# An attention block and a channel mix on one core: the opening reordered, one operand loaded instead of computed, all stores in quarters

## The chip, the cores and the metric

One Trainium2 chip, one of its cores. A core has five engines with queues of their own: TensorE (PE, with its weight loads shown as PEld), VectorE (DVE), ScalarE (ACT), GpSimd (POOL) and SyncE (SP). SP, ACT and POOL can issue DMAs. The metric is the device time of one execution in microseconds, a median over runs.

## The reference

Four batches, four heads, 1088 positions, 32 numbers a head. `S1` and `S2` are 8 x 32.

```python
def phi(x):                                   # 64 features of a position
    a = einsum('rd,bhsd->bhsr', S1, x)
    b = einsum('rd,bhsd->bhsr', S2, x)
    return einsum('bhsi,bhsj->bhsij', a, b).reshape(*x.shape[:-1], 64)
q_p, k_p = phi(q), phi(k)
kv  = einsum('bhsf,bhsd->bhfd', k_p, v)
z   = sum(k_p, axis=2)
num = einsum('bhsf,bhfd->bhsd', q_p, kv)
den = einsum('bhsf,bhf->bhs', q_p, z)[..., None] + 1e-06
x   = (num / den), heads side by side         # (4, 1088, 128)

x_prev = x shifted by one position, zero first
xk = mu_k * x + (1 - mu_k) * x_prev
xr = mu_r * x + (1 - mu_r) * x_prev
k  = maximum(xk @ w_k, 0)                     # 128 -> 1024
out = sigmoid(xr @ w_r) * (k * k @ w_v)       # 1024 -> 128
```

## The kernel before

The scheduling is by hand. A text, `ORDER`, lists some 365 tasks; a loop at the end (L601) calls the function of each name in that order, and each engine then works through its own instructions strictly in the order in which they were written. So moving a word in `ORDER` moves that task on its engine's queue, and no other thing plans the work. The parts of a word: `abw.1.0.W@0` is task `abw` for batch 1, half 0, in form `W`, into PSUM bank 0. A last letter A, V or G names ACT, DVE or POOL (in `st` also S for SP); `^sq.1.3.V` adds a wait for that earlier task. Waits follow from the data, PSUM banks included.

The tasks by batch `b`, in the order of the data:

- `kturn.b.y` (DVE, L262) transposes half `y` of k in blocks of 32; `smk`/`sevk` (PE L209, DVE L213) build `SK`, a block form of S1 and S2; `kproj.b.j` (PE, L273) projects k, in form P with 32 columns an instruction or W with 64; `abev` copies to SBUF; `kp.b.j.G` (POOL, L255) makes the 64 features; `kvmm` (PE, L321) sums features times v, then `kvev`, `kdmm`, `kvcp` turn the sums.
- `zmm`, `zev`, `wmm`, `wsq` (PE L300, copy, PE L308, DVE L312) make the denominators' weights from the projections of k, with an operand `ZL`. `ZL` is S1 spread over 128 partitions times a mask: `smz` (PE, L201) spreads S1 by a product with `ez`, and `sevz` (DVE, L204) applies the mask.
- `qturn.b` (DVE, L344) transposes q; `abw.b.g` (PE, L353 and L367; P or W) projects it in two halves, with the denominators' part; `abwev` copies; `pw` (POOL), `dred` (DVE, L393), `drec` (DVE, L398) and `an` (POOL) make and apply the denominators; `qp.b.g` (DVE) makes q's features.
- Batch 0 turns them on PE (`qt`, L473, copied by `qtev`; `qtt`, `qttev`, `xt`, `xtev` for a rest of two positions) and multiplies by kv in `xmh` (PE, L485; copied by `xev`). Batches 1 to 3 turn them on DVE (`qf`, L420) and use `xmm` (PE, L433).
- `xs` (POOL, L498) fills the shifted rows, `xk` and `xkt` (DVE, L505, L464) mix x with x_prev into bf16, `xb` (POOL, L252) makes the other mix's input. `wkc`, `wrc`, `wvc` (POOL) make the bf16 weights; `mumm` and `wmu` turn the mu vectors into columns.

The channel mix runs in nine groups, two a batch (0 to 7) and group 8 of half the size for the rests. `f1.g.c` (PE, L526) makes a quarter of the 1024 hidden rows, two products of 128x512; `relu` (L534 on ACT, L536 on DVE) and `sq` (L546 on ACT, L255 elsewhere) follow; `f2.g.c` (PE, L558) multiplies back; `rr` (PE, L571) and `sig` (ACT, L576) make the gate; `fin` (DVE, L581) multiplies; `st` (L595) stores 256 KB a group, either whole or in quarters of 32 partitions (64 KB).

`zz.n` (PE, L188) issues `n` products of a zero tile with 512 columns of zeros; nothing reads their result.

All loads are issued ahead, on SP but for the first S1 and k half and the two mu rows, which are on ACT, in the order of `LOADS`.

Of the kernel before, what the change touches and what calls it, by code (L numbers as in the profile page):

```python
# [44 lines left out]
kvmm.3.0@5 abwev.3.1.A qf.1.2 relu.1.0.A pw.3.2.G^sq.0.1.V kdmm.1 f1.1.1@01 kvcp.1.A f1.0.3@34 sq.1.0.G relu.1.1.A
kvmm.3.1 dred.3.2.V kproj.2.0.P@6 relu.0.3.A kvev.3.V drec.3.2 kdmm.3 abev.2.0.V rr.0@0 sq.0.2.A an.3.2.G kvcp.3.V
zmm.2@1 kp.2.0.G qp.3.0 xmm.1@3456 sig.0 zev.2.A sq.1.1.A qp.3.1 wmm.2 f2.0.0@7 xev.1.0.A f2.0.1 xtev.1.A wsq.2
xev.1.1.V rr.1@0 sq.1.2.A xs.1 f1.1.3@12 sq.0.3.V abw.2.0.W@3 xk.1.2 relu.1.3.A abw.2.1.W@4 abwev.2.0.A sig.1 sq.1.3.V
f1.3.0@56 abwev.2.1.A qf.3.2 f2.0.2 relu.3.0.A pw.2.2.G^sq.1.3.V f1.2.0@01 f2.1.0@2 xb.1.G^sq.1.3.V relu.2.0.A
f1.3.1@56 f2.0.3 relu.3.1.A f2.1.1 dred.2.2.V f1.3.2@01 fin.0 st.0.S sq.3.0.A f1.2.1@56 drec.2.2 relu.3.2.V f2.1.2  # L50
an.2.2.G relu.2.1.A f2.1.3 kp.2.1.G kvmm.2.0@7 qp.2.0 sq.3.2.A xmm.3@0156 sq.2.0.A fin.1 st.1.S sq.3.1.G qp.2.1
kvmm.2.1 xev.3.0.A f1.3.3@23 xev.3.1.A xtev.3.V f2.3.0@4 kvev.2.V relu.3.3.A xs.3 f1.2.2@56 xk.3.2 f1.2.3@01
relu.2.2.A f2.3.1 rr.3@2 sq.2.1.V relu.2.3.A kdmm.2 f1.6.0@56 sq.2.2.V f2.3.2 relu.6.0.A sq.3.3.V f1.6.1@01 qf.2.2
f2.2.0@3 sq.2.3.G^sq.3.3.V sig.3 f2.3.3 relu.6.1.A f1.7.0@56 f2.2.1 relu.7.0.A rr.2@2 xb.3.G f1.6.2@01 fin.3 st.3.S
kvcp.2.A f2.2.2 relu.6.2.A xmm.2@4567 sq.6.0.V sig.2 sq.7.0.V sq.6.1.V f2.2.3 xev.2.0.A f2.6.0@2 sq.6.2.V xtev.2.A
f1.7.1@01 xev.2.1.A fin.2 st.2.S xs.2^sq.6.2.V f2.6.1 relu.7.1.A xk.2.2 f1.7.2@67 rr.6@3 relu.7.2.A f1.6.3@45 sq.7.1.V
f1.7.3@01 sig.6 f2.6.2 sq.7.2.G^sq.7.1.V relu.7.3.V relu.6.3.A f1.5.0@67 f2.7.0@3 f2.7.1 relu.5.0.A f1.5.1@01 sq.6.3.V
f1.5.2@45 relu.5.1.A rr.7@6 sq.7.3.V f2.6.3 sq.5.0.V sig.7 f1.4.0@01 relu.5.2.V f2.7.2 sq.5.1.G^sq.5.0.V relu.4.0.A
f2.7.3 f1.5.3@67 fin.6 st.6.S sq.5.2.A f1.4.2@45 relu.5.3.V f1.4.1@12 xb.2.G relu.4.2.A f2.5.0@0 f2.5.1 fin.7 st.7.S
relu.4.1.A f1.4.3@67 sq.5.3.V f1.8.0@45 f2.5.2 sq.4.0.V relu.8.0.A f1.8.2@12 f2.5.3 relu.4.3.A sq.4.1.V rr.5@3  # L60
sq.4.2.V rr.8@4 relu.8.2.A f2.4.0@5 sq.8.0.V f1.8.1@67 sig.5 sq.4.3.V f2.4.1 relu.8.1.A f1.8.3@12 sq.8.2.V rr.4@3
fin.5 st.5.0.S st.5.1.S st.5.2.S relu.8.3.A sq.8.1.G^sq.8.2.V f2.4.2 sig.4 f2.4.3 sq.8.3.A f2.8.0@0 fin.4 st.4.0.S
st.4.3.S f2.8.1 sig.8 f2.8.2 f2.8.3 fin.8 st.8.2.S st.5.3.G st.4.1.A st.4.2.G st.8.0.A st.8.1.G st.8.3.A
# [583 lines left out]
```

## Time and profile before

| | |
|---|---|
| median of 3 runs | 81.73 us (81.45 to 82.52) |
| profiled execution | 82.54 us |
| its span, first to last instruction | 80.7 us |
| PE busy | 74.1 us (92%) |
| DVE busy | 65.4 us (81%) |
| ACT busy | 56.0 us (69%) |
| POOL busy | 47.4 us (59%) |
| zero products | 18, 7.7 us |
| HBM read, written | 7.80 MB, 2.23 MB |

Three stretches can be told apart in the slices of the page. Up to some 27 us loads fill the DMA engines and attention of batch 0 and half of that of batches 1 and 3 is made; from there to about 76 the channel mix runs, with what is left of attention between its products; then the last stores land. In a row of the timeline, the first two numbers are the start and the length in microseconds, then engine, line, operation, output<-input, form and count; in brackets stands how long the engine had been idle and what ended that. A row can cover several instructions of the same kind that followed one another. Lines of the chain of waits give start, length and what the time went to.

### The profile page before, as it was taken

The numbers are of one execution on the slowest core, as the hardware profiler recorded it, in microseconds if no ns is written. First come the engines' busy times: TensorE is split into PE (matmuls) and PEld (weight loads), VectorE is DVE, ScalarE is ACT, GpSimd is POOL, SyncE is SP. The second block draws the span as 40 slices with busy tenths as digits, with TensorE's granted clock in tenths as the row PEclk, the third lists the DMA queues.
The fourth block names the chain that finished last, engine by engine and source line by source line (L and its number), as shares of the span: only waits on it lengthen the run. The fifth ranks groups of instructions, "written<-read, shape, count | busy, mean of one in ns | idle before, by whom it ended". The sixth has DMA issues, their size and how long they took to land.

```text
span 80.7 us, 3273 instructions
## 1 busy us (share of the span) xinstructions
PE 74.1 (92%) x1410; PEld 52.2 (65%) x1410; DVE 65.4 (81%) x102; ACT 56.0 (69%) x88; POOL 47.4 (59%) x68
## 2 busy tenths in 40 slices
...
PEclk9999999999999999999999999999999999999995
...
GB/s 20 312 349 307 292 337 362 231 263 310 382 299 245 181 9 0 8 0 12 0 0 12 0 15 71 83 86 24 0 27 96 55 89 0 15 51 109 176 238 5
DMA packets 7258, 10.24 MB, mean 127 GB/s; under 512 B 762, under 2 KB 4060, under 8 KB 7244
## 3 DMA queue, kind: packets, MB, share of 16 engines
...
q10 hardware_dynamic: 308, 0.41, 1.5%
q8 instruction: 11, 0.18, 0.9%
q0 software_dynamic: 96, 0.16, 0.8%
...
HBM read 7.80 MB, written 2.23 MB: 124 GB/s over the span
## 4 chain that ended last, share of the span: by engine, by line
PE 61%; POOL 12%; DVE 10%; ACT 6%; issue 4%; POOLq 1%; ACTq 0%
PE ps L526 13%; PE ps L558 12%; PE ps L188 8%; PE ps L433 6%; PE ps L367 6%; POOL kp L255 5%; PE ps L273 5%; ACT k L534 5%; PE ps L321 3%; DVE k L536 3%; PE ps L571 3%; DVE osb L581 2%; DVE XK L505 2%; DVE k L255 2%; POOL pw L255 1%
## 5 line engine op out<-in xcount | busy, mean ns | idle before, releaser
L534 ACT ACTIVATE k<-ps 128x1024 bf16<-128x1024 f32 (+1 forms) x32 | 29.7, 976 | 1.1 <-DVE XK L505 0.3
L558 PEld LDWEIGHTS <-k 128*128 128x128 bf16 x272 | 16.9, 98 | 4.2 <-issue 0.5
L526 PE MATMUL ps<-XK,wk 128*128 128x512 bf16 (+1 forms) x72 | 19.2, 367 | 0.2 <-DVE XK L464 0.2
L558 PE MATMUL ps<-wv,k 128*128 128x128 bf16 x272 | 19.1, 219 | 0.0
L255 POOL TENSOR_TENSOR kp<-ab 128x1280 f32<-128x1280 f32 (+1 forms) x8 | 17.3, 2178 | 1.0 <-ACT ab L248 1.0
L255 POOL TENSOR_TENSOR k<-k 128x1024 bf16<-128x1024 bf16 (+1 forms) x6 | 10.5, 1751 | 11.8 <-DVE k L255 9.2
L255 DVE TENSOR_TENSOR k<-k 128x1024 bf16<-128x1024 bf16 (+1 forms) x21 | 14.1, 708 | 0.3 <-PE ps L558 0.3
L255 DVE TENSOR_TENSOR qp<-an,ps 128x1152 f32<-128x1152 f32 (+1 forms) x8 | 10.1, 1269 | 0.0
L546 ACT ACTIVATE k<-k 128x1024 bf16<-128x1024 bf16 (+1 forms) x9 | 9.1, 1028 | 0.4 <-PE ps L558 0.3
L188 PE MATMUL ps<-zero 128*128 128x512 bf16 x18 | 7.7, 560 | 1.2 <-DVE warm L155 1.2
L262 DVE STREAM_TRANSPOSE kT<-k 128x576 f32<-128x576 f32 x8 | 5.9, 753 | 3.1 <-DMA k<-in_k_dram 3.1
L526 PEld LDWEIGHTS <-wk 128*128 128x128 bf16 x72 | 6.1, 98 | 3.3 <-issue 0.7
L255 POOL TENSOR_TENSOR pw<-abw 128x272 f32<-128x272 f32 (+2 forms) x5 | 3.3, 650 | 7.6 <-ACT abw L248 7.6
L420 DVE STREAM_TRANSPOSE qf<-qp 128x2176 f32<-128x2176 f32 x3 | 7.3, 2435 | 0.0
L248 ACT COPY ab<-ps 128x256 f32<-128x256 f32 (+1 forms) x7 | 2.7, 396 | 6.1 <-PE ps L273 5.9
L367 PE MATMUL ps<-SQ,qT 128*64 128x96 f32 (+1 forms) x144 | 6.6, 250 | 0.0
L581 DVE TENSOR_TENSOR osb<-ps,r 128x512 f32<-128x512 f32 (+1 forms) x9 | 5.8, 648 | 0.9 <-ACT r L576 0.5
L273 PEld LDWEIGHTS ps<-SK,kT 128*32 128x32 f32 (+1 forms) x200 | 5.3, 145 | 1.4 <-issue 0.8
L273 PE MATMUL ps<-SK,kT 128*32 128x64 f32 (+1 forms) x200 | 6.1, 256 | 0.0
L248 ACT COPY X<-ps 128x512 f32<-128x512 f32 (+2 forms) x12 | 4.9, 434 | 1.8 <-PE ps L485 1.2
L367 PEld LDWEIGHTS ps<-SQ,qT 128*64 128x64 f32 (+1 forms) x144 | 5.5, 131 | 0.5 <-DVE SQ L312 0.3
L321 PE MATMUL ps<-kp,v 128*32 128x64 f32 x288 | 5.7, 222 | 0.0
...
## 6 DMA issues: line engine op xcount, KB each, us to landing
...
```

Source lines behind the costliest of these rows:

```text
L188: nc.tensor.matmul(PS[:, banks[0], :], zero[:, :P], zero[:], skip_group_check=True)
L248: nc.scalar.copy(o, i)
L255: (nc.vector if eng == "V" else nc.gpsimd).tensor_mul(o, a, b)
L273: nc.tensor.matmul(_ap(d, [[n, 2], [1, 32]]), sb["kT", b][:, m, w * c:w * c + w], SK[:, :, :H].rearrange("p x h r -> p x (h r)"), skip_gro ...
L321: nc.tensor.matmul(o[32 * h:32 * h + 32, :F], vin[b][:, h, m, :], sb["kp", b, j][:, 4 * (m - KG[j][0]) + h].rearrange("p i j -> p (i j)"), ...
L367: nc.tensor.matmul(o[32 * w * c:32 * w * c + 32 * w, n:n + 96], sb["qT", b][:, u:u + w, :].rearrange("p u a -> p (u a)"), SQ[b][:, x:x + H ...
L420: nc.vector.transpose(sb["qf", b][:, s0:s1].rearrange("p s f a -> p (s f a)"), sb["qp", b][:, s0:s1].rearrange("p s i j -> p (s i j)"))
L526: nc.tensor.matmul(h[:, c, :], wk[:, P * (2 * cp + c):P * (2 * cp + c) + P], x, skip_group_check=True)
L534: nc.scalar.activation(o, h, RELU)
L546: nc.scalar.activation(o, i, SQUARE)
L558: nc.tensor.matmul(o[:, i * P:i * P + P], k2[:, i * P:i * P + P], wv[:, 2 * cp + c, :], start=(cp == 0 and c == 0 and i == 0), stop=(cp == ...
L581: nc.vector.tensor_mul(o[:].rearrange("p i f -> p (i f)")[:, :n], ps["o", g][:, :n], sb["r", g][:, :n])
```

## The change

- S1 is also loaded once more, read sixteen times over into a tile `SZ` of 128 partitions, by a DMA on ACT's queue behind the first k half and ahead of the mu rows. `sevz` reads `SZ`; the product `smz`, its operand `ez` and the copy that made `ez` go.
- The zero tile has 128 columns instead of 512; the zero product reads it four times over, so that it still has 512 columns. The zero products stand elsewhere: `zz.6 zz.1 zz.4 zz.3 zz.1 zz.3` before, `zz.6 zz.2 zz.1 zz.3 zz.2 zz.4` after.
- `qturn.0` comes before `sevz` and both `kturn.1`, and `abw.0.0` before `kproj.1`.
- The stores of groups 0, 1, 2, 3, 6 and 7 are issued in quarters on SP; those of 5, 4 and 8 were already.
- `ORDER` is new from end to end, with other PSUM banks. Up to the first f1, by engine: DVE `kturn.0.0 kturn.0.1 sevk qturn.0 sevz kturn.1.0 kturn.1.1 wsq.0 dred.0.0 drec.0.0 dred.0.1 qp.0.0 drec.0.1 qturn.1 wsq.1 wmu qp.0.1 kturn.2.0 kturn.2.1 qttev.0 dred.1.2 drec.1.2 qturn.2 kturn.3.0 kturn.3.1 xkt.0 xk.0.0 xk.0.1`; POOL `kp.0.0 kp.0.1 pw.0.0 pw.0.1 an.0.0 kp.1.0 an.0.1 wkc pw.1.2 kp.1.1 wrc wvc an.1.2 xs.0 xb.0`.
- On another engine: ACT to DVE `qttev.0 zev.2 sq.3.0 kvcp.2 relu.8.0`; DVE to ACT `kvev.3 kvev.2 relu.3.2 relu.5.2`; POOL to DVE `sq.7.2 sq.8.1 sq.2.3`; POOL to ACT `sq.3.1`; ACT to POOL `sq.3.2 sq.8.3`; DVE to POOL `sq.2.2`. `kproj.2.0` and `abw.3.0` change from form P to W, `kproj.2.1` from W to P.

```diff
 ORDER = """
-kturn.0.0 zz.6@1 smk@0 smz@1 kturn.0.1 sevk sevz zz.1@2 kproj.0.0.P@0 sqc.2 sqc.1 sqc.0 sqc.3 kproj.0.1.P@1 abev.0.0.A
-kp.0.0.G kturn.1.0 abev.0.1.A zz.4@2 zmm.0@0 kturn.1.1 zev.0.A zz.3@2 wmm.0 qturn.0 kproj.1.1.W@1 kproj.1.0.W@2
-kp.0.1.G wsq.0 zz.1@3 abw.0.0.W@0 abev.1.0.A abev.1.1.A zmm.1@1 abwev.0.0.A abw.0.1.W@2 zev.1.A pw.0.0.G mumm@3
-dred.0.0.V abwev.0.1.A kvmm.0.0@4 drec.0.0 pw.0.1.G qturn.1 an.0.0.G kp.1.1.G qp.0.0 wmm.1 kvmm.0.1 kvev.0.A
-dred.0.1.V zz.3@7 qt.0.0@56 wmu wsq.1 kdmm.0 drec.0.1 qtev.0.0.A abw.1.1.W@3 kturn.2.0 an.0.1.G wrc qtt.0@1 qp.0.1
-abw.1.0.W@0 qttev.0.A kp.1.0.G kvcp.0.A xt.0 kturn.2.1 abwev.1.0.A qt.0.1@45 abwev.1.1.A xtev.0.A xmh.0.0@2 qturn.2
-qtev.0.1.A pw.1.2.G wkc.G xmh.0.1@4 dred.1.2.V drec.1.2 kproj.2.1.W@5 xs.0 kturn.3.0 xev.0.1.A wvc.G kvmm.1.0@6
-abev.2.1.A kturn.3.1 xev.0.0.A an.1.2.G xk.0.0 xb.0.G kproj.3.1.W@5 xkt.0 kproj.3.0.W@7 xk.0.1 abev.3.1.A f1.0.0@12
...
+kturn.0.0 zz.6@1 smk@0 kturn.0.1 sevk zz.2@1 kproj.0.0.P@0 sqc.2 sqc.1 sqc.3 sqc.0 qturn.0 kproj.0.1.P@1 abev.0.0.A
+kp.0.0.G abev.0.1.A sevz kturn.1.0 zz.1@2 zmm.0@0 kturn.1.1 zev.0.A zz.3@2 wmm.0 mumm@1 wsq.0 kp.0.1.G zz.2@2
+abw.0.0.W@0 kproj.1.0.W@2 abwev.0.0.A abw.0.1.W@3 abev.1.0.A pw.0.0.G kproj.1.1.W@4 dred.0.0.V abwev.0.1.A drec.0.0
+pw.0.1.G abev.1.1.A an.0.0.G dred.0.1.V zz.4@5 zmm.1@2 kp.1.0.G qp.0.0 kvmm.0.0@4 zev.1.A kvmm.0.1 drec.0.1 qturn.1
+qtt.0@0 wmm.1 kvev.0.A qt.0.0@56 an.0.1.G wsq.1 wmu kdmm.0 abw.1.0.W@7 qtev.0.0.A qp.0.1 wkc.G abw.1.1.W@1 abwev.1.0.A
+kturn.2.0 qt.0.1@23 abwev.1.1.A kvcp.0.A pw.1.2.G kturn.2.1 kvmm.1.0@4 qtev.0.1.A kp.1.1.G qttev.0.V dred.1.2.V
+drec.1.2 qturn.2 xt.0 xmh.0.1@2 wrc kproj.2.1.P@3 wvc.G xmh.0.0@5 kturn.3.0 abev.2.1.A xtev.0.A an.1.2.G xev.0.1.A
+kturn.3.1 xev.0.0.A xs.0 xkt.0 kproj.3.1.W@3 xk.0.0 xb.0.G kproj.3.0.W@0 xk.0.1 abev.3.1.A f1.0.0@56 abev.3.0.A
...
+    SZ = const.tile([P, D], F32)
...
-    zero = const.tile([P, 512], BF16)
+    zero = const.tile([P, P], BF16)
...
+    nc.scalar.dma_start(SZ[:], dataclasses.replace(S1, ap=[[0, P // R], [D, R], [1, D]]))
...
-    ez = const.tile([R, 16, R], F32)
-    nc.vector.tensor_copy(ez[:], _ap(ident[:R, :R], [[0, 16], [1, R]]))
...
-            nc.tensor.matmul(PS[:, banks[0], :], zero[:, :P], zero[:], skip_group_check=True)
+            nc.tensor.matmul(PS[:, banks[0], :], zero[:], _ap(zero[:], [[0, 4], [1, P]]), skip_group_check=True)
...
-    def smz(banks):
-        ps["sz"] = PS[:, banks[0], :D]
-        nc.tensor.matmul(ps["sz"], ez[:].rearrange("r g j -> r (g j)"), S16[:R, :], skip_group_check=True)
...
-        nc.vector.tensor_mul(ZL[:], _ap(ps["sz"], [[0, 4], [1, D]]), _ap(mz[:], [[1, 4], [0, D]]))
+        nc.vector.tensor_mul(ZL[:], _ap(SZ[:], [[0, 4], [1, D]]), _ap(mz[:], [[1, 4], [0, D]]))
```

More of the change, by code (lines that the diff above doesn't have):

```diff
@@ L40 @@
-abw.1.0.W@0 qttev.0.A kp.1.0.G kvcp.0.A xt.0 kturn.2.1 abwev.1.0.A qt.0.1@45 abwev.1.1.A xtev.0.A xmh.0.0@2 qturn.2
-qtev.0.1.A pw.1.2.G wkc.G xmh.0.1@4 dred.1.2.V drec.1.2 kproj.2.1.W@5 xs.0 kturn.3.0 xev.0.1.A wvc.G kvmm.1.0@6
-abev.2.1.A kturn.3.1 xev.0.0.A an.1.2.G xk.0.0 xb.0.G kproj.3.1.W@5 xkt.0 kproj.3.0.W@7 xk.0.1 abev.3.1.A f1.0.0@12
-qp.1.0 kp.3.1.G abev.3.0.A f1.0.2@45 relu.0.0.A zmm.3@7 kvmm.1.1 zev.3.V qturn.3 relu.0.2.A wmm.3 kp.3.0.G f1.1.2@01
-sq.0.0.A f1.0.1@45 wsq.3 kvev.1.V abw.3.0.P@7 qp.1.1 relu.0.1.A abw.3.1.W@2 abwev.3.0.V relu.1.2.A sq.0.1.V f1.1.0@34
@@ L45 @@
[L45 to L63, printed above, removed]
+kturn.0.0 zz.6@1 smk@0 kturn.0.1 sevk zz.2@1 kproj.0.0.P@0 sqc.2 sqc.1 sqc.3 sqc.0 qturn.0 kproj.0.1.P@1 abev.0.0.A
@@ new lines @@
+drec.1.2 qturn.2 xt.0 xmh.0.1@2 wrc kproj.2.1.P@3 wvc.G xmh.0.0@5 kturn.3.0 abev.2.1.A xtev.0.A an.1.2.G xev.0.1.A
+kturn.3.1 xev.0.0.A xs.0 xkt.0 kproj.3.1.W@3 xk.0.0 xb.0.G kproj.3.0.W@0 xk.0.1 abev.3.1.A f1.0.0@56 abev.3.0.A
+qturn.3 kp.3.1.G f1.0.2@23 relu.0.0.A zmm.3@0 kvmm.1.1 zev.3.V qp.1.0 relu.0.2.A wmm.3 f1.1.2@56 kp.3.0.G sq.0.0.A
+f1.0.1@23 wsq.3 kvev.1.V abw.3.0.W@0 qp.1.1 relu.0.1.A abw.3.1.W@7 relu.1.2.A abwev.3.0.V f1.1.0@12 sq.0.1.V kdmm.1
+abwev.3.1.A qf.1.2 f1.1.1@56 relu.1.0.A pw.3.2.G^sq.0.1.V kvmm.3.0@3 kvcp.1.A kvmm.3.1 sq.1.0.G relu.1.1.A f1.0.3@12
```

22 lines of the change are left out of this document (21 added, 1 removed).

## The prediction

> **What bounds the kernel now.** I read the page first: span, granted clock, the chain that ended last.
>
> ```profile
> span 80.7 us, 3273 instructions
> ...
> PEclk9999999999999999999999999999999999999995
> ...
> PE 61%; POOL 12%; DVE 10%; ACT 6%; issue 4%; POOLq 1%; ACTq 0%
> ```
>
> The chain is PE's for 61% of the span. The busy times by stage say where something else shares the limit (columns: stretch and its length, then busy us and count of PE, PEld, DVE, ACT, POOL).
>
> ```profile
> 27.00:65.00 38.00, 37.85 (x803) 26.77 (x803) 37.30 (x48) 36.28 (x52) 23.19 (x23) 1.00 0.12 33
> 65.00:75.00 10.00, 10.00 (x139) 8.52 (x138) 9.57 (x15) 9.50 (x14) 4.14 (x5) 1.00 0.18 53
> ```
>
> From the first f1 on, PE has 0.15 us free, DVE and ACT 2 to 5% of the time, POOL some 40%. An order can therefore win little there: only what shortens PE's own list, or lets that list begin sooner. So the beginning decides. The timeline, cut to the steps that count (start, length, engine, line, form, idle before):
>
> ```profile
> 5.22 2.15 PE L273 MATMUL ps<-SK,kT 128*32 128x64 f32 x72
> 6.58 0.42 ACT L248 COPY ab<-ps 128x320 f32<-128x320 f32 x1 [2.69 <-PE ps L273]
> 7.26 0.78 DVE L262 STREAM_TRANSPOSE kT<-k 128x576 f32<-128x576 f32 x1 [1.91 <-DMA k<-in_k_dram]
> 7.29 1.89 PE L188 MATMUL ps<-zero 128*128 128x512 bf16 x4
> 7.43 0.37 ACT L248 COPY ab<-ps 128x256 f32<-128x256 f32 x1 [0.43 <-PE ps L273]
> 9.11 0.53 PE L300 MATMUL ps<-ab 128*32 128x32 f32 x18
> 9.13 1.27 DVE L344 STREAM_TRANSPOSE qT<-q 128x1088 f32<-128x1088 f32 x1
> 9.57 1.24 PE L188 MATMUL ps<-zero 128*128 128x512 bf16 x3
> 10.90 1.27 PE L273 MATMUL ps<-SK,kT 128*64 128x64 f32 x36
> 11.01 0.21 DVE L312 TENSOR_TENSOR SQ<-ps,m 128x48 f32<-128x48 f32 x1 [0.61 <-PE ps L308]
> 12.42 0.32 PE L353 MATMUL ps<-SQ,qT 128*64 128x48 f32 x4
> 14.47 0.38 PE L220 MATMUL ps<-ident,mu_row 2*128 2x2 f32 x2
> 16.41 0.82 PE L188 MATMUL ps<-zero 128*128 128x512 bf16 x3
> 17.55 1.09 PE L473 MATMUL ps<-ident,qp 128*128 128x128 f32 x8 [0.32 <-DVE qp L255]
> 22.05 2.23 PE L485 MATMUL ps<-qf,kvr 64*32 64x512 f32 x16
> 24.22 0.69 PE L273 MATMUL ps<-SK,kT 128*64 128x64 f32 x16
> 24.83 0.77 PE L321 MATMUL ps<-kp,v 128*32 128x64 f32 x40
> 25.27 0.59 ACT L248 COPY X<-ps 128x512 f32<-128x512 f32 x1
> 25.96 0.75 DVE L505 SCALAR_TENSOR_TENSOR XK<-ps,rat,X 128x512 bf16<-128x512 f32 x1 [0.59 <-POOL wv L244]
> 26.96 1.25 PE L526 MATMUL ps<-XK,wk 128*128 128x512 bf16 x4 [0.16 <-DVE XK L464]
> 35.12 0.74 PE L273 MATMUL ps<-SK,kT 128*32 128x64 f32 x40
> ```
>
> Two things stand in it. First, PE's list is nearly full already from abw.0.0 (12.42) to the end of the second xmh (22.05 + 2.23 = 24.28). Second, the clock: three zero products took 1.24 us at 9.57 and 0.82 at 16.41, and the first k projections 2.15/72 = 30 ns each where those of batch 2 took 0.74/40 = 18.5. PE was slow up to about 10 and fast later; the PEclk row, all nines there, doesn't show it.
>
> **The change, part by part. Up to abw.0.0.** The wait for the second ab copy ends at 7.43 + 0.37 = 7.80. Before, four zero products (1.89 us, behind the projections) kept zmm.0 back to 9.11; now one does, so zmm.0 starts at 7.85, 1.26 earlier. zz.3 stays between it and wmm.0, so wsq.0 moves from 11.01 to 9.75. At the pace of the four, three would take 1.42 and not 1.24: PE turned fast during them, some 10.4 us into the span, and earlier ones will be slow throughout, so I add 0.2: 9.95. Behind wmm.0, PE now has mumm (0.38) and two zero products (0.41 each). abw.0.0 starts at about 10.9 instead of 12.42.
>
> The moved qturn.0 (1.27) is hidden: q is loaded ahead of the k half that landed at 7.26, so at worst qturn.0, sevz and both kturn.1 follow one another from 7.26 (1.27 + 0.21 + 0.78 + 0.78, sevz put at wsq.0's price) to 10.3, still before the zero products end. kproj.1 and kturn.1 lose nothing, as their products now stand behind abw.0.0. The removed sz product and ez copy free PE and DVE of work, but kproj.0.0 waited for SK, behind the second kturn, so it stays at 5.22: nothing. The replicated S1 load puts one issue on ACT's queue, ahead of the two mu loads and the table load; ACT then idles 2.69 us before its first copy, which covers it. SZ is read some 5 us after its issue; if it came later, kturn.1 and wmm.0 would wait behind sevz. I take nothing. mumm's loads have 8 us and more. The smaller zero tile saves a part of a memset before any load has landed: nothing; the repeated view streams the same 512 columns as f1's strided one.
>
> The title's "fewer zero products" I cannot find: 6+1+4+3+1+3 = 18 before, 6+2+1+3+2+4 = 18 after. Only ahead of abw.0.0 it is 14 against 15. They move; they aren't saved.
>
> **PE from abw.0.0 to f1.** Before, 24.28 − 12.42 = 11.86 us. Out go mumm (0.38), the three zero products (0.82) and the 0.32 of idle before qt.0.0. In come four zero products (4 × 0.27 = 1.09, if fast), kproj.1 (1.27), kvmm.1.0 (0.77) and kproj.2.1 (0.69), which the new order puts ahead of the last xmh: 11.86 − 1.52 + 3.82 = 14.16. From 10.9 that ends at 25.06. The ACT copy of x.0.0 (0.59) ends at 25.7. Then xk.0.0 needs only xs.0 as well, which is POOL's:
>
> ```profile
> 15.85 1.95 POOL L255 TENSOR_TENSOR kp<-ab 128x1024 f32<-128x1024 f32 x1
> 19.36 0.37 POOL L237 TENSOR_SCALAR wr<-wr_f,mu 128x128 bf16<-128x128 f32 x1
> 22.41 0.76 POOL L255 TENSOR_TENSOR pw<-abw 128x272 f32<-128x272 f32 x1
> 24.37 1.03 POOL L244 CAST wv<-wv_f 128x1024 bf16<-128x1024 f32 x1
> 25.38 0.64 POOL L255 TENSOR_TENSOR an<-abw,den 128x272 f32<-128x272 f32 x1
> ```
>
> The new order puts pw.1.2, kp.1.1, wrc (two like the 0.37), wvc and an.1.2 ahead of xs.0. pw.1.2 waits for abw.1.1, which ends before qt.0.1, kvmm.1.0, both xmh and kproj.2.1: 25.06 − 1.09 − 0.77 − 2.23 − 0.69 = 20.3, and an ACT copy, 20.65. Adding 0.76 + 1.95 + 0.74 + 1.03 + 0.64 = 5.12 gives 25.8, and behind xs.0, a copy of 31 columns put at 0.15, xk.0.0 starts at 25.95, as before. What was won early is spent again on PE and POOL. The one gain left: xkt, which stood between xk.0.0 and f1.0.0, is now ahead of both, so f1.0.0 comes at 26.65, **0.3 us** earlier.
>
> **After f1.** abw.3.0 changes to the wide form. The chain has both forms, each with its second half:
>
> ```profile
> 30.64 1.61 PE ps L367 x48
> ...
> 40.95 1.33 PE ps L367 x32
> ```
>
> PE gets 0.28 back there; kvev.3 moves off DVE in the same stretch. kproj.2.0 and 2.1 swap forms and cancel (36 wide ones took 1.27, 40 narrow ones 0.74 for half a batch). I take **0.25 us**. Of the other tasks that change engine most are swaps of two like ones; these are not:
>
> ```profile
> L534 ACT ACTIVATE k<-ps 128x1024 bf16<-128x1024 f32 (+1 forms) x32 | 29.7, 976 | 1.1 <-DVE XK L505 0.3
> L255 POOL TENSOR_TENSOR k<-k 128x1024 bf16<-128x1024 bf16 (+1 forms) x6 | 10.5, 1751 | 11.8 <-DVE k L255 9.2
> L255 DVE TENSOR_TENSOR k<-k 128x1024 bf16<-128x1024 bf16 (+1 forms) x21 | 14.1, 708 | 0.3 <-PE ps L558 0.3
> 62.87 1.22 DVE L536 TENSOR_SCALAR k<-ps 128x1024 bf16<-128x1024 f32 x1
> ```
>
> relu.3.2 and relu.5.2 go to ACT (+0.98 each; DVE −1.22 each); sq.3.0, sq.7.2, and relu and one square of the half-size group 8 go to DVE (0.71 + 0.71, and some 0.6 + 0.4 as half of the full-size rows). ACT also gives up a square of group 8. Each balance is within 0.5 us of zero; POOL loses one square (1.75), and has room. No gain in sum.
>
> **Stores in quarters.** SP's queue has nothing else to do by then. A quarter's issue on it, and the products that set free group 6's store and group 5's:
>
> ```profile
> L595 SPq DMA_DIRECT2D out_dram<-osb x12: 314/475/642, 46.1 to 77.6; - x12
> ...
> 67.80 0.67 DVE L581 TENSOR_TENSOR osb<-ps,r 128x512 f32<-128x512 f32 x1
> ...
> 73.90 0.68 DVE L581 TENSOR_TENSOR osb<-ps,r 128x512 f32<-128x512 f32 x1
> ```
>
> The eight of groups 6 and 7 take 8 × 0.475 = 3.8 us of SP, and those products were 6.1 us apart. Hidden; were they closer than 3.8 us, every microsecond less would hold up the last stores by one. The stores of groups 5, 4 and 8 are in quarters already, and what lies behind the last product stays.
>
> **Clock, the open price.** The order takes three slow zero products out of the stretch in which PE turned fast. [...] I take no loss, since the new order has PE without a gap from 7.85 on; the other end is rival A.
>
> **Sum.** −0.3 − 0.25 = −0.55 us on the span, 80.7 to 80.15. The profiled execution took 82.54 with 1.84 around its span, so 82.0; it lies 0.8 above the median of 81.73. Carried to the median: **81.2**, with 80.6 to 81.8 for this case alone.
>
> **Rivals.** *A, slower: PE stays slow until the four zero products behind kproj.1 have run.* Place: 10.4 to about 15.6. Slow projections cost 30 against 18.5 ns, so 5.2 us of slow work do 3.2 us' worth; 2.0 us are lost on a list with no slack, and up to 2.6 if the ratio is 2, as of a doubled clock. It decides once abw.0.0 ends later than 12.4. 81.2 + 2.1 = 83.3 (82.4 to 84.2). For it: nine zero products instead of eleven before zmm.0. Against: no gap behind them.
>
> *B, faster:* the new distribution also removes DVE's 0.43 and ACT's 0.5 us of idle between 65 and 75, where both are as full as PE. 81.2 − 0.9 = 80.3 (79.8 to 80.6). Against it: all three engines must fit at once.
>
> *C, later at the end:* relu.5.2 puts 0.98 us on ACT, which has 0.5 free between 65 and 75, and what it gives up (group 8) comes only afterwards. +0.6, and as much again if DVE waits: 82.3 (81.8 to 82.9).
>
> *D:* quarter stores queue on SP past group 5's product, if it comes within 3.8 us of group 6's: at 2.4 us apart +1.4, 82.6. [...]
>
> **Chances.** Forecast 0.55, A 0.15, B 0.12, C 0.14, D 0.04. 2% is 1.6 us, about what a measurement of this kernel can tell: faster means under 80.1, slower over 83.4. Faster: half of B and the forecast's lowest edge, 0.10. Slower: half of A and the edges of C and D, 0.11. Same: 0.79. The range takes B's middle and A's lower half: 80.1 to 83.4.
>
> **What would show it.** zmm.0 near 7.9 and abw.0.0 near 10.9; the four zero products near 14 in 1.1 us (A: 1.9); xs.0 as the last thing before xk.0.0, and f1.0.0 at 26.3 to 26.9; xmm.1 about 0.5 us earlier than before. I am wrong if f1.0.0 comes before 25.5 or after 28, if DVE or ACT idle by a microsecond more after 30, or if SP still issues group 7's quarters when group 5's product is done.

## The result

The changed kernel took 84.94 us (median of 4, 84.74 to 85.22), the kernel before 82.12 beside it (81.45 to 83.34). The ratio is 1.037, with a 95% interval of 1.028 to 1.047: slower, and above the forecast range (80.1 to 83.4). The profiled execution took 84.74, its span 83.0 against 80.7. One execution of a kernel may lie several per cent above its own fastest (81.23 to 84.47 for the kernel before on one chip); ratios here leave such disturbed ones out ("none" where too few were left), medians take all, and a profile is one execution.

The page of the changed kernel: span, granted clock, and the chain by engine.

```profile
span 83.0 us, 3259 instructions
...
PEclk9999999999999999999999999999999999999997
...
PE 66%; DVE 11%; DMA 6%; ACT 5%; POOL 4%; issue 2%; ACTq 1%; POOLq 1%; DVEq 0%
```

DMA now stands in the chain with 6%, and the page puts it down to k's loads. Before it had no share.

The busy times by stage, with the stretches moved by 1 us as f1 begins later (columns as before):

```profile
28.00:66.00 38.00, 37.23 (x763) 26.49 (x761) 36.27 (x49) 35.95 (x51) 21.88 (x24) 1.00 0.15 38
66.00:76.00 10.00, 10.00 (x141) 8.48 (x139) 9.23 (x16) 9.71 (x14) 2.41 (x4) 1.00 0.23 56
```

PE still has nothing free towards the end, and 0.77 us in the first 38. The timeline of the changed kernel at the steps that count, opening first:

```profile
1.77 0.63 ACTq L171 DMA_DIRECT2D SZ<-in_S_dram  x1
...
5.97 0.78 DVE L259 STREAM_TRANSPOSE kT<-k 128x576 f32<-128x576 f32 x1 [1.64 <-DMA k<-in_k_dram]
...
6.95 2.15 PE L270 MATMUL ps<-SK,kT 128*32 128x64 f32 x72 [2.02 <-DVE SK L210]
...
9.56 0.53 PE L297 MATMUL ps<-ab 128*32 128x32 f32 x18
...
11.94 0.32 PE L350 MATMUL ps<-SQ,qT 128*64 128x48 f32 x4
...
14.58 1.04 PE L189 MATMUL ps<-zero 128*128 128x512 bf16 x4
...
18.97 1.12 POOL L231 TENSOR_SCALAR wk<-wk_f,omu 128x1024 bf16<-128x1024 f32 x1 [0.71 <-DVE omu L223]
...
19.10 0.99 DVE L225 TENSOR_TENSOR rat<-tmp,mu 128x1 f32<-128x1 f32 x1
...
21.27 1.09 PE L470 MATMUL ps<-ident,qp 128*128 128x128 f32 x8 [1.21 <-DVE qp L252]
...
25.79 0.21 POOL L495 COPY X<-X 128x31 f32<-128x31 f32 x1 [0.24 <-ACT X L245]
...
27.67 1.25 PE L523 MATMUL ps<-XK,wk 128*128 128x512 bf16 x4 [0.28 <-DVE XK L502]
...
29.53 0.35 PE L297 MATMUL ps<-ab 128*32 128x32 f32 x18 [0.61 <-ACT k L531]
...
37.97 1.91 PE L430 MATMUL ps<-qf,kvr 32*32 32x288 f32 x64
...
77.44 0.42 DVE L578 TENSOR_TENSOR osb<-ps,r 128x256 f32<-128x256 f32 x1 [0.36 <-PE ps L555]
```

And rows of the kernel before that answer to some of these and were not shown yet:

```profile
18.45 0.16 DVE L228 TENSOR_TENSOR rat<-tmp,mu 128x1 f32<-128x1 f32 x1
...
36.97 1.60 PE L433 MATMUL ps<-qf,kvr 32*32 32x288 f32 x64
...
76.16 0.42 DVE L581 TENSOR_TENSOR osb<-ps,r 128x256 f32<-128x256 f32 x1 [0.37 <-PE ps L558]
```

The 2.3 us of span split at two marks, f1.0.0 and fin.8 (the last product, half-size group 8):

| | before | after | difference |
|---|---|---|---|
| start to f1.0.0 | 26.96 | 27.67 | +0.71 |
| f1.0.0 to fin.8 | 49.20 | 49.77 | +0.57 |
| fin.8 to the end of the span | 4.54 | 5.56 | +1.02 |

Three things strike the eye. The second k half of batch 0 is turned at 5.97 (the projections behind it began at 5.22 before and at 6.95 now). A product of 128 numbers, rat, took 0.99 us instead of 0.16, and ended with POOL's wkc (18.97 + 1.12 = 20.09); behind it came qp.0.1, and PE was without work for 1.21 us. And the end is a microsecond longer, although the same four stores lie behind fin.8.

### The profile page after: what moved, and what is told of

It reads as the page before. It is cut to its first block, busy times and chain, and to the rows that moved or that the text cites. A ratio compares the mean times of both kernels' runs of the same rounds, so it can differ in the third digit from the quotient of the medians.

```text
span 83.0 us, 3259 instructions
## 1 busy us (share of the span) xinstructions
PE 71.9 (87%) x1388; PEld 51.2 (62%) x1388; DVE 65.1 (78%) x104; ACT 55.9 (67%) x86; POOL 45.3 (55%) x67
## 4 chain that ended last, share of the span: by engine, by line
PE 66%; DVE 11%; DMA 6%; ACT 5%; POOL 4%; issue 2%; ACTq 1%; POOLq 1%; DVEq 0%
PE ps L523 17%; PE ps L555 16%; PE ps L430 6%; DMA k<-in_k_dram 6%; PE ps L270 5%; PE ps L364 5%; DVE qp L252 5%; PE ps L568 4%; PE ps L318 3%; PE ps L189 2%; DVE qT L341 1%; ACT X L245 1%; PE ps L297 1%; POOL out_dram L592 1%; PE ps L470 1%
## 5 line engine op out<-in xcount | busy, mean ns | idle before, releaser
L531 ACT ACTIVATE k<-ps 128x1024 bf16<-128x1024 f32 (+1 forms) x33 | 30.9, 992 | 1.9 <-PE ps L523 1.1
L252 DVE TENSOR_TENSOR k<-k 128x1024 bf16<-128x1024 bf16 (+1 forms) x24 | 14.7, 650 | 0.4 <-PE ps L555 0.3
L252 POOL TENSOR_TENSOR k<-k 128x1024 bf16<-128x1024 bf16 (+1 forms) x5 | 8.6, 1724 | 10.6 <-DVE k L252 7.6
L249 POOL CAST XB<-X 128x288 bf16<-128x288 f32 (+1 forms) x8 | 4.8, 629 | 6.8 <-DVE k L252 5.9
L189 PE MATMUL ps<-zero 128*128 128x512 bf16 x18 | 7.0, 512 | 1.0 <-DVE warm L158 1.0
L543 ACT ACTIVATE k<-k 128x1024 bf16<-128x1024 bf16 x7 | 7.4, 1079 | 0.4 <-PE ps L555 0.4
L364 PE MATMUL ps<-SQ,qT 128*64 128x96 f32 x128 | 6.2, 247 | 0.0
L573 ACT ACTIVATE r<-ps 128x512 f32<-128x512 f32 (+1 forms) x9 | 5.3, 586 | 0.4 <-DVE osb L578 0.4
L364 PEld LDWEIGHTS ps<-SQ,qT 128*64 128x64 f32 x128 | 5.5, 137 | 0.0
L318 PE MATMUL ps<-kp,v 128*32 128x64 f32 x288 | 5.2, 221 | 0.0
```

The lines of the kernel that those rows point to most:

```text
L189: nc.tensor.matmul(PS[:, banks[0], :], zero[:], _ap(zero[:], [[0, 4], [1, P]]), skip_group_check=True)
L252: (nc.vector if eng == "V" else nc.gpsimd).tensor_mul(o, a, b)
L318: nc.tensor.matmul(o[32 * h:32 * h + 32, :F], vin[b][:, h, m, :], sb["kp", b, j][:, 4 * (m - KG[j][0]) + h].rearrange("p i j -> p (i j)"), ...
L364: nc.tensor.matmul(o[32 * w * c:32 * w * c + 32 * w, n:n + 96], sb["qT", b][:, u:u + w, :].rearrange("p u a -> p (u a)"), SQ[b][:, x:x + H ...
L531: nc.scalar.activation(o, h, RELU)
L543: nc.scalar.activation(o, i, SQUARE)
```

## The experiments

Theory 1 puts the loss on three separate hold-ups: the SZ load, DVE waiting for POOL, the quarter stores. Theory 2 is that the new order itself is slower, or that the clock's phase made it look so. Each kernel was run beside the kernel before on the same chip: ten executions of the changed kernel without SZ, of that with the late SZ load, of the kernel before with SZ, with four SZ loads and filled; four of the others. So a median over all executions and a ratio can disagree, and differences of some 1% between two rows are not told apart.

| run | median, us | kernel before, same chip | ratio, 95% interval |
|---|---|---|---|
| changed kernel again | 84.87 | 82.96 | 1.027 [1.017, 1.037] |
| changed, no SZ load | 84.05 | 83.03 | 1.000 [0.993, 1.007] |
| before, with SZ load | 83.55 | 83.03 | 1.005 [0.991, 1.018] |
| before, with four SZ loads | 83.62 | 82.76 | 1.012 [1.000, 1.024] |
| changed, whole stores | 84.55 | 83.03 | 1.016 [1.008, 1.023] |
| before, quarter stores | 84.81 | 83.68 | 1.025 [0.989, 1.062] |
| changed, wmu earlier | 84.96 | 83.03 | none |
| changed, rat from the products' bank | 84.02 | 82.96 | 1.013 [0.998, 1.028] |
| changed, SZ load behind the table load | 85.36 | 82.96 | 1.013 [1.002, 1.025] |
| changed, four things undone | 84.32 | 82.96 | none |
| changed, three things undone | 84.75 | 83.68 | none |
| the same, filled | 83.17 | 83.68 | 1.012 [0.991, 1.034] |
| the same, filled, with SZ load | 85.49 | 82.76 | 1.024 [1.009, 1.039] |
| before, filled | 82.63 | 82.76 | 1.000 [0.991, 1.010] |

**The SZ load, taken away and put in.** One kernel is the changed one with SZ no longer loaded (the sz product and the ez copy are back), the other the kernel before with SZ loaded.

```diff
 changed kernel, no SZ load
-    nc.scalar.dma_start(SZ[:], dataclasses.replace(S1, ap=[[0, P // R], [D, R], [1, D]]))
-        nc.vector.tensor_mul(ZL[:], _ap(SZ[:], [[0, 4], [1, D]]), _ap(mz[:], [[1, 4], [0, D]]))
+        nc.vector.tensor_mul(ZL[:], _ap(ps["sz"], [[0, 4], [1, D]]), _ap(mz[:], [[1, 4], [0, D]]))
-... smk@0 kturn.0.1 sevk ...
+... smk@0 smz@7 kturn.0.1 sevk ...
```

> The new order without the replicated load of S1; the product that spreads S1 is back (into bank 7). Load theory (the 128 short rows of that load, on ACT's queue right behind the first batch's second k half, hold that half up): the second kturn of batch 0 starts at about 4.3 again and not at 5.97, the first k projection at 5.2 and not 6.95; the clock then turns later against the work, so that only some 1.0 of the 1.7 us reaches the first f1 (26.6 to 26.9, was 27.67). Time about 83.9, ratio 1.02 to 1.03 against before. Rival, chance or crowding by the long loads: the second kturn stays near 6 and the time near 84.9.

> The kernel before with one part of the change alone: S1 loaded replicated, the spreading product and its operand gone, order otherwise as before. Load theory: the second kturn at about 6.0 (was 4.3), the first k projection at 6.9 (was 5.22), everything up to f1 later by 1.0 to 1.7 us, time 82.8 to 83.6, ratio 1.01 to 1.02. Rival: no change, ratio 1.00.

Without the load the changed kernel's second turn began at 4.50 and f1.0.0 came at 25.35, earlier than forecast. With the load in the old order they came at 5.08 and 27.00 (4.28 and 26.96 without), so the load theory's 6.0 and 1.0 to 1.7 us missed there. Without the load the changed kernel is level with the one before by the ratio (1.000), which rests on three of its ten executions; over all ten the median is still 1.02 us above. With the load the old order loses 0.5%, which is not to be told from nothing. So the load seems to cost the new order more than the old, and a later second k half is unlikely to be all of it. It isn't even a sure part: that half's turn began at 4.3 to 5.5 us in eight kernels without the load or with a late one, and at 4.6 to 6.0 in those with it. So that SZ held this half up in the profiled run is not shown.

**The load stream, by dose.** Three more copies of SZ, which nobody reads, are loaded behind the first in the kernel before.

```diff
 kernel before with SZ
+    SZX = [const.tile([P, D], F32, name=f"szx{i}") for i in range(3)]
+    nc.scalar.dma_start(SZX[0][:], dataclasses.replace(S1, ap=[[0, P // R], [D, R], [1, D]]))
+    nc.scalar.dma_start(SZX[1][:], dataclasses.replace(S1, ap=[[0, P // R], [D, R], [1, D]]))
+    nc.scalar.dma_start(SZX[2][:], dataclasses.replace(S1, ap=[[0, P // R], [D, R], [1, D]]))
```

> The kernel before with the SZ load four times (three of the copies are read by nobody), against one copy in the earlier run (sixth megabyte landed at 22.4 us, f1.0.0 at 27.00, 83.55 us) and none (22.1, 26.96). If each replicated load takes the load stream some 0.5 to 1 us: the sixth megabyte lands at 24 to 26 us, f1.0.0 comes at 28 to 30 us behind turns that wait for k, and the time is 1.5 to 3 us above the kernel before. If the load costs nothing and the spread is chance: f1.0.0 at 27.0 to 27.3 and the time within 0.6 us of the run with one copy.

The stretch from 4 to 10 us by the windows view (its last column is GB/s moved): kernel before, changed kernel, four copies.

```profile
4.00:10.00 6.00, 6.00 (x107) 3.54 (x104) 3.71 (x7) 1.01 (x3) 3.80 (x6) 1.00 0.99 315
```

```profile
4.00:10.00 6.00, 3.98 (x93) 2.42 (x92) 3.99 (x7) 1.50 (x4) 2.08 (x5) 1.00 0.75 247
```

```profile
4.00:10.00 6.00, 3.43 (x83) 2.36 (x81) 2.31 (x6) 2.28 (x4) 1.74 (x5) 1.00 0.72 219
```

And the timeline with four copies, the second turn and f1.0.0:

```profile
6.30 0.78 DVE L262 STREAM_TRANSPOSE kT<-k 128x576 f32<-128x576 f32 x1 [1.97 <-DMA k<-in_k_dram]
...
28.80 1.25 PE L526 MATMUL ps<-XK,wk 128*128 128x512 bf16 x4 [0.16 <-DVE XK L464]
```

In these 6 us the loads moved 275 to 315 GB/s in seven profiles without SZ, 247 to 280 in seven with one copy right behind the loads, and 219 with four. A copy is only 16 KB, in rows of 128 bytes. With four copies f1.0.0 came at 28.80 instead of 26.96, as forecast (28 to 30), but the time rose by only 1.2% (0 to 2.4%) where I had 1.5 to 3 us. The dose points to a load that slows the stream, but it is one profile with four copies, of an execution of 84.32 us where the median was 83.62. One copy is some 24 GB/s in the mean (290 against 266), which is 0.5 us of these 6, and the two groups overlap: its cost to the stream is an estimate, not shown.

> The SZ load is issued on ACT's queue behind the table load instead of right behind the second k half. If its 128 small rows hold up that half: the second turn of batch 0 starts at 4.2 to 4.6 us (5.97 and 4.6 to 5.1 in the three other runs with the early load), f1.0.0 comes up to 0.7 us sooner than in the changed kernel, and ZL is still there before wmm.0. If the second half is late for another reason, its start lies anywhere from 4.3 to 6.0 and the time does not change; if SZ now comes late, PE waits for ZL before wmm.0.

```diff
 changed kernel, SZ load behind the table load
-    nc.scalar.dma_start(SZ[:], dataclasses.replace(S1, ap=[[0, P // R], [D, R], [1, D]]))
     nc.scalar.dma_start(mu_row[:1, :], moe_mu_k.rearrange("(x d) -> x d", x=1))
     nc.scalar.dma_start(mu_row[1:, :], moe_mu_r.rearrange("(x d) -> x d", x=1))
     nc.scalar.activation(warm[:], warm[:], SIGMOID)
+    nc.scalar.dma_start(SZ[:], dataclasses.replace(S1, ap=[[0, P // R], [D, R], [1, D]]))
```

The second turn began at 5.31, not at 4.2 to 4.6: a miss, and another sign that the half's lateness is not that queue's order. The fastest executions came down to 82.94, the median of the ten rose to 85.36 (one took 139.5): moving the load did not mend it.

**DVE's operations that wait for POOL.** rat is the product of tmp and mu, both in SBUF. Here its second operand is read from the bank of the mu product; POOL's wkc stays where it was.

```diff
 changed kernel, rat from the products' bank
-        nc.vector.tensor_mul(rat[:], tmp[:], mu[:, :1])
+        nc.vector.tensor_mul(rat[:], tmp[:], ps["mu"][:, :1])
```

> rat's second operand is read from the products' bank and no longer from the copy, so that only one operand comes from SBUF; POOL's wkc still runs at the same moment. If an operation of DVE with two operands in SBUF has to wait for POOL's, rat falls from 0.99 to about 0.16 us, qp.0.1 starts 0.8 us sooner, PE's wait before qt.0.1 falls from 1.21 to about 0.4 us, and abw.0.0 to f1.0.0 from 15.7 to about 15.0 us: 0.5 to 0.8 us less in all. If POOL's presence alone slows DVE, rat stays near 1 us and the time is that of the changed kernel.

The timeline of this kernel, POOL and DVE, then PE and the next thing that is late:

```profile
18.71 1.12 POOL L231 TENSOR_SCALAR wk<-wk_f,omu 128x1024 bf16<-128x1024 f32 x1 [0.70 <-DVE omu L223]
...
18.84 0.15 DVE L225 TENSOR_TENSOR rat<-tmp,ps 128x1 f32<-128x1 f32 x1
...
20.18 1.09 PE L470 MATMUL ps<-ident,qp 128*128 128x128 f32 x8 [0.25 <-DVE qp L252]
...
24.83 1.58 DVE L259 STREAM_TRANSPOSE kT<-k 128x576 f32<-128x576 f32 x2 [1.03 <-DMA k<-in_k_dram]
```

0.15 us with wkc still beside it (18.71 + 1.12 = 19.83), against 0.99 where rat ended with wkc: it was not POOL's presence that held rat, but its two operands in SBUF at the same time. PE's wait for qp.0.1 fell from 1.21 us to 0.25, further than forecast (0.4). The median fell by 0.85 us against the changed kernel beside it (forecast 0.5 to 0.8), but that it was rat's is not shown: there were four executions of each (83.34 to 86.51 against 84.54 to 85.47), and f1.0.0 came at 27.66, no earlier than in the changed kernel's first profile (27.67; the rerun's opening, 28.91, differs for another reason, below), since the turns of batch 3 now waited 1.03 us for k's load. Here the loads set the opening.

The kernel before had such a wait in its trace, far from the opening: a square on DVE, two operands in SBUF, took 1.53 us from 64.00 where its neighbours took 0.68, beside a square on POOL that ended at 64.99.

The same hold, which an expectation further down calls the lock, is a part of what the SZ load costs the new order.

> The changed kernel as it is, beside the kernels below on one chip. Theory 1 (three separate hold-ups: the SZ load in front of the first k halves, rat beside POOL's wkc, a code load behind the quarter stores): 84.0 to 85.2 us, rat at about 1 us again, a fourth code load of 8192 bytes behind the last store. Theory 2 (the new order is as good as the old one and its 3% was the clock's phase in those runs): a median within 1 us of the kernel before, with spans scattered as widely.

It took 84.87, 1.91 above the kernel before, so the loss is not the chance of one comparison; rat took 0.99 again, and the fourth code load stood at the end.

The changed kernel when it was run again, first the granted clock by slices, then the timeline (POOL's kp.0.0 and kp.0.1, ZL, PE behind it, products of abw, and part of kvmm.1.0):

```profile
PEclk9999965999999999999999999999999999999998
```

```profile
7.00 4.35 POOL L252 TENSOR_TENSOR kp<-ab 128x1280 f32<-128x1280 f32 x2 [0.45 <-ACT ab L245]
...
7.56 1.99 DVE L201 TENSOR_TENSOR ZL<-SZ,mz 128x128 f32<-128x128 f32 x1
...
9.70 0.39 PE L305 MATMUL ps<-zs,ZL 128*128 128x48 f32 x2 [1.31 <-DVE ZL L201]
...
11.34 1.56 PE L364 MATMUL ps<-SQ,qT 128*64 128x96 f32 x16
...
24.02 0.65 PE L318 MATMUL ps<-kp,v 128*32 128x64 f32 x31 [0.59 <-issue]
```

Before, ZL was made from the sz product in a bank of PSUM; now both its operands, SZ and mz, lie in SBUF, and turning q first puts it where kp.0.0 already runs (the first of the two POOL operations in the row, 7.00 to 9.40). ZL took 1.99 us, to 9.55, instead of some 0.25, and PE stood 1.31 us; later the granted clock fell (the 6 and the 5 in the PEclk row; half from 11.16 to 14.57) and 16 products of abw took 1.56 us instead of 0.85. In the changed kernel without SZ, ZL lies beside the same POOL work and is not held:

```profile
6.82 4.31 POOL L257 TENSOR_TENSOR kp<-ab 128x1280 f32<-128x1280 f32 x2 [0.45 <-ACT ab L250]
...
7.69 0.25 DVE L206 TENSOR_TENSOR ZL<-ps,mz 128x128 f32<-128x128 f32 x1
```

In the changed kernel's first profile this did not show: its k came late (5.97) and its first projections were slow (2.15), so that ZL (8.04) was done before kp.0.0 had begun (8.82). The seven profiles of the changed order with SZ divide that way: the first projections took 1.21 us in three, and ZL was held in all three (1.71, 1.74 and 1.99); they took 2.15 in four, and ZL took 0.25 in all four. So with SZ this order gives back what a fast start of PE wins. With fast projections and a held ZL f1.0.0 came at 28.30, 28.78 and 28.91; with fast projections and no SZ, in two profiles, at 25.35 and 26.64.

wmu right behind wsq.0, ahead of its old place, moves rat away from wkc:

```diff
-... mumm@1 wsq.0 kp.0.1.G ...  wsq.1 wmu kdmm.0 ...
+... mumm@1 wsq.0 wmu kp.0.1.G ...  wsq.1 kdmm.0 ...
```

> The changed kernel with the six small DVE steps of the mu vectors (1.8 us there, 0.99 of it one product of 128x1 that ended with POOL's weight conversion) moved to where DVE idles, behind wsq.0. If they were on the path: the second half of q's features of batch 0 starts at 18.3 (was 20.01), the second transposes of q's features on PE at 20.1 (was 21.27) and without PE's 1.2 us of idle before them, the first f1 at 26.5 to 27.0 (was 27.67), time 83.9 to 84.3, ratio 1.025 to 1.03. If POOL's copies or the wait for xs bound as well: f1 unchanged, 84.9. On the side: if a DVE product with two inputs in SBUF waits for a running POOL instruction that reads SBUF, the two such products here end when POOL's features of batch 0 end, near 13.1; if the 0.99 belonged to the weight conversion alone, each takes 0.16.

It didn't help (84.96). rat took 0.16 us and PE no longer waited ahead of the second qt, which began at 19.17; but in this profile the turns of batch 3 waited 1.21 us for k's load, PE waited for them, and f1.0.0 came at 29.12. And the hold took another operation with two operands in SBUF, the sum of omu and tmp, 0.80 us instead of 0.16, beside POOL's kp (7.55 + 4.37 = 11.92, and 11.13 + 0.80 = 11.93):

```profile
7.55 4.37 POOL L252 TENSOR_TENSOR kp<-ab 128x1280 f32<-128x1280 f32 x2 [0.97 <-ACT ab L245]
...
11.13 0.80 DVE L223 TENSOR_TENSOR omu<-omu,tmp 128x1 f32<-128x1 f32 x1
```

**Quarter stores.** Whole stores in the changed kernel for the groups whose stores the change had split, and quarter stores in the kernel before:

```diff
 changed kernel, whole stores (groups 0, 1, 2, 3, 6, 7)
-... fin.0 st.0.0.S st.0.1.S st.0.2.S st.0.3.S ...
+... fin.0 st.0.S ...
 kernel before, quarter stores (the same groups)
-... fin.0 st.0.S ...
+... fin.0 st.0.0.S st.0.1.S st.0.2.S st.0.3.S ...
```

> The changed kernel with the stores of groups 0, 1, 2, 3, 6 and 7 whole again. The prediction's step (quarters are hidden): 84.9, ratio 1.037, and the same tail, 5.5 us from the last product's start to the end. Rival (quarters on SP or in the DMA engines hold up the last stores): 0.5 to 1.0 us less, 84.0 to 84.4, with the tail back to 4.5 us.

> The kernel before with the stores of groups 0, 1, 2, 3, 6 and 7 in quarters, and nothing else. If quarter stores bring a fourth code load of 8192 bytes behind the last store: that load is there, from the last store's end to the span's end it is about 2.4 to 2.7 us instead of 1.8, and the time is 0.4 to 0.8 us above the kernel before. If the load belongs to the new order: three such loads and no difference. SP's issues still end before group 5's product in both.

The changed kernel took 84.55 with whole stores, and 4.96 from the last product to the end: between the two forecasts. The page's rows for the instruction queue 14: kernel before, changed, kernel before with quarters.

```profile
q14 instruction: 3, 0.02, 0.1%
```

```profile
q14 instruction: 4, 0.03, 0.2%
```

```profile
q14 instruction: 4, 0.03, 0.1%
```

The fourth packet is 8 KB of code, and its record lies behind everything else: in the changed kernel it begins at 82.46 and ends at 83.03, at the span's end, while the last data had moved at 80.28. Every kernel with quarter stores has it there (five others of the changed order too), none with whole stores; where two kernels with whole stores count four packets, the fourth is of 96 bytes and lies at the span's start. In the old order, f1.0.0 to fin.8 stayed at 49.20 with quarters, and fin.8 to the end grew from 4.54 to 5.33: 0.8 us, without any store that waits for another. In the changed order the end took 5.2 to 5.6 us with quarters (six profiles) and 4.7 to 5.1 with whole stores (five); one order alone scattered by 0.6 there. The last part tells them apart best: from the last data moved to the span's end it is 2.3 to 2.7 us in the seven profiles with quarters and 1.6 to 2.2 in the nine with whole stores. So quarters cost 0.4 to 0.8 us, by the profiles; the times (1.016 for whole stores against 1.027, in different comparisons) agree without proving it. That the code load is what takes this time, and not something else that 18 more stores bring, fits its place at the very end but is not shown.

**All undone at once.** No SZ load, rat from the bank, whole stores; and once more with group 5's gate, sigmoid, product and stores moved forward in the order and the last square on ACT:

```diff
 four things undone, beside the three: the end of the order
-rr.4@4 ... sq.4.1.V relu.4.3.A ... rr.5@3 ... sig.5 ... fin.5 st.5.0.S st.5.1.S st.5.2.S sig.4 sq.8.3.G^sq.8.2.V
+rr.5@4 ... sq.4.1.V sig.5 fin.5 st.5.0.S st.5.1.S st.5.2.S relu.4.3.A ... rr.4@3 ... sig.4 sq.8.3.A
```

> The changed order with four things undone: no SZ load (the sz product is back), rat from the products' bank, whole stores for groups 0, 1, 2, 3, 6 and 7, and at the end group 5's sigmoid and product ahead of group 4's and the last square on ACT. Theory 1: the parts add up (0.7 + 0.7 + 0.6 + 0.5) and the time is 81.5 to 82.5, at or below the kernel before on the same chip; no fourth code load. Theory 2: no gain beyond 0.5 us against the changed kernel.

> The changed order with no SZ load (the sz product is back), rat from the products' bank and whole stores; the end of the order is the changed kernel's. If DVE's two waits for POOL (ZL, rat) and the code load were the loss: 82.5 to 83.3, within 0.5 us of the kernel before, ZL 0.25 us and rat 0.16 us. If the order itself loses more (PE waiting for its code or its clock): 84 or more, as the run with four things undone showed (84.3), with PE's gaps put down to nothing in the profile.

Neither came out as theory 1 had it. The four gave 84.32, the three 84.75 with a spread from 82.95 to 86.72. ZL and rat took 0.25 and 0.15 to 0.16 us in both, as expected, and no fourth code load stood at the end; still the time was not back. Both profiles have PE waiting for nothing that the profile shows inside kvmm.1.0 or the first f1 (1.32 us and 0.77); and the first projections were slow (2.15), as in the changed kernel. The parts don't simply add up.

**Filled.** The same three undone, with two more zero products in the gap ahead of the first projection; then with the SZ load again; and the filling alone in the kernel before.

```diff
-... kturn.0.1 sevk zz.2@1 kproj.0.0.P@0 ...
+... kturn.0.1 sevk zz.4@1 kproj.0.0.P@0 ...
```

> The same with two more zero products ahead of the first k projection, in the 0.4 to 2 us in which PE waits for the second k half. [...] If the clock's phase is chance: no difference, or up to 0.5 us more where k comes early.

> The filled version (changed order, rat from the products' bank, whole stores, two more zero products) with the replicated SZ load kept. Without it: 83.17 us beside 83.68 of the kernel before. If SZ costs by the lock and the load stream: ZL 1.7 to 2 us whenever POOL's kp.0.0 is running, PE 1 to 1.3 us without work before wmm.0, and 84.0 to 85.0 us. If it is harmless: 83.0 to 83.5 beside the same kernel before, ZL 0.25 us.

> The kernel before with two more zero products ahead of the first k projection, nothing else. [...] If the opening's later part is bound by the loads or by PE's own list: no change, or 0.4 us more for the two products.

The filled version: first projections, a turn that waits for k, f1.0.0.

```profile
6.03 1.21 PE L272 MATMUL ps<-SK,kT 128*32 128x64 f32 x72 [0.53 <-DVE SK L212]
...
23.09 1.48 DVE L261 STREAM_TRANSPOSE kT<-k 128x576 f32<-128x576 f32 x2 [1.00 <-DMA k<-in_k_dram]
...
26.64 1.02 PE L525 MATMUL ps<-XK,wk 128*128 128x512 bf16 x4 [0.75 <-DVE XK L504]
```

And the same with SZ (ZL, PE behind it, PE at kvmm.1.0):

```profile
7.72 1.71 DVE L198 TENSOR_TENSOR ZL<-SZ,mz 128x128 f32<-128x128 f32 x1
...
9.58 0.39 PE L302 MATMUL ps<-zs,ZL 128*128 128x48 f32 x2 [1.31 <-DVE ZL L198]
...
23.85 0.69 PE L315 MATMUL ps<-kp,v 128*32 128x64 f32 x33 [1.45 <-issue]
```

Filled, the new order is back at the old one's time (83.17 beside 83.68; 1.012, from 0.991 to 1.034), with fast projections from the start; and PE, quick now, waits for the loads of batch 3, so that f1.0.0 comes at 26.64. Putting SZ back takes the median from 0.5 us below the kernel before to 2.7 above it, with ZL held for 1.71 us; but these are four executions each on two chips, the profile is of the longest of its four (87.48), and the intervals of the two ratios overlap. The old order gains nothing from the filling (1.000; its first projections took 2.15 us in that profile, as without it), so the filling alone is no gain; the 1.6 us between the medians of the new order with three things undone, filled and unfilled, rest on four executions each, and I don't call them shown. No version beat the kernel before by more than the scatter.

Taken together: by the medians the changed order with SZ in its place lies 1.1 to 2.8 us above the kernel before in six comparisons, without SZ 1.4 above to 0.5 below in four; f1.0.0 came at 27.66 to 29.12 in the six profiles with, at 25.35 to 28.22 in the four without. The ranges overlap.

## Why the prediction was wrong

**Up to abw.0.0** fell at the step "I take nothing" for the replicated load. It was costed as an issue on ACT's queue, which was right (0.63 us, covered), and as a possible late arrival; not as a burden on the loads beside it, and not as a change of where ZL reads from, which is what the runs show: ZL 1.71 to 1.99 us instead of 0.25 and PE 1.31 us without work, wherever the first projections were fast. In the profiled run ZL was not held. There zmm.0 came at 9.56 instead of 7.85 and abw.0.0 at 11.94 instead of 10.9, because "it stays at 5.22" failed: the first projection began at 6.95, behind the late k half, and whether SZ or chance made that half late is open. With SZ gone abw.0.0 came at 9.53, 10.19, 11.13 and 12.14 in four profiles, on both sides of the forecast; so the rest of that step, the zero products and the order, is neither shown nor refuted.

**PE from abw.0.0 to f1** hit its number by two errors that cancel. The windows of that stretch, before and after (from abw.0.0 to the end of the second xmh):

```profile
12.42:24.28 11.86, 11.40 (x214) 7.66 (x215) 8.91 (x20) 4.90 (x13) 8.57 (x11) 1.00 1.08 305
```

```profile
11.94:26.11 14.17, 12.80 (x321) 9.38 (x321) 11.17 (x22) 5.89 (x14) 11.58 (x14) 1.00 1.03 312
```

14.17 us against 14.16 forecast; but PE was busy for 12.80. The sum of durations was 1.4 us too long (a group's duration runs into the next one's: in the kernel before, the 0.69 us from 24.22 end behind 24.83, where the next begins), and the missing 1.37 were two waits, 1.21 for qp.0.1 and 0.16. That is luck. The first wait is mostly rat's: of wkc, moved forward on POOL to where wmu runs, I counted no cost, and did not look which operands wmu reads meanwhile. xs.0 came at 25.79, where the sum had 25.8, and that is luck too: it waited for ACT, not for POOL's list, and xk.0.0 waited for ACT's copy of x.0.0, behind an xmh that ended at 26.11. f1.0.0 came at 27.67, 1.0 later than forecast, which is what abw.0.0 was late.

**After f1**: the 0.25 us did not come. The wide form of abw.3.0 saved its 0.28, and xmm.1 took 1.90 to 1.93 instead of 1.60, in all eleven profiles of the new order and in none of the five of the old; why is open. f1.0.0 to fin.8 was 49.06 to 49.41 in six profiles of the new order and 49.6 to 51.9 in five, 49.20 to 49.42 in five of the old: the profiled run had 0.61 us of PE's idle time at zmm.3 in it, which most don't have. That the engines' swaps balance fits these figures. So rivals B and C are out: no gain between 65 and 75, and PE stayed full to the end.

**Stores in quarters**: hidden on SP, as said, and rival D is out: group 5's product came 9.8 us behind group 6's (75.63 and 65.85), too far apart to queue. But "what lies behind the last product stays" fell: 4.54 to 5.56, of which quarters make 0.4 to 0.8. "Hidden" was weighed by SP's issue time alone. The fourth code load, which came with the 18 more stores (82.46 to 83.03), was left out.

**Clock**: that a list without a gap loses nothing was an estimate. In the profiled run PE turned fast at the three zero products ahead of wmm.0 (0.98 us for the three), as in the kernel before (1.24), and the four at 14.58 took 1.04: rival A as put is refuted there. In the rerun PE was fast first and slow again after the wait for ZL: half the clock was granted for 3.4 us there (11.16 to 14.57), and likewise in both other profiles with a held ZL, where 16 products of abw took 1.54 us. Ahead of it PE had waited 1.31 us in all three. That this wait was the cause is not shown: a pause of 1.45 us at 22.40 in the filled kernel with SZ was followed by no fall before 31.44.

So the failed step is the nothing for SZ, with two more that were not in the sum: the hold on rat and the longer end behind quarter stores. Of some 1.9 to 2.8 us lost, quarters are 0.4 to 0.8 by the profiles, and SZ 0.9 by the medians (1.02 above the kernel before without it, 1.91 with it, on two chips), more by the ratios (1.000 against 1.027). For rat the operation's 0.84 us and most of PE's wait are shown; what they are worth in time is not, as the loads of batch 3 took over in both profiles that were rid of them and kept SZ and quarters. The three overlap: undone together without filling they gave back little, so the sum of the loss stays in part unexplained. What PE waits for inside kvmm.1.0 is open.
